# Regrouping the block visits of a fused SwiGLU stage, with a lower initial pace of weight conversion

## The chip, the cores and the metric

The kernel runs on one core of one Trainium2 chip. The metric is device time in microseconds. Three runs of the kernel before took 545.49, 545.72 and 546.81 us; the median is 545.72 us. One further execution was profiled: it took 543.5 us, of which 541.7 us lie between its first and its last instruction (the span). All times of rows below are microseconds from the start of that span.

## The reference, cut to what matters

Three layers follow each other. The first two (chunked attention with a softmax inside each chunk, then a soft mixture of experts) fill the first third of the kernel and are not touched. The third is a SwiGLU layer on 4608 tokens with 512 features and 1536 hidden features:

```python
def _moe2_ref(x, w_gate, w_val, w_out):
    g = x @ w_gate
    silu = g * (1.0 / (1.0 + np.exp(-g)))
    val = x @ w_val
    return (silu * val @ w_out).astype(np.float32)
```

Its x is the output of the mixture, `c @ slot_out` with only 32 slots. The kernel therefore never forms x: it multiplies `slot_out` with the weights once and then works from the 32 combine weights of each token.

## The kernel before, in words

**Blocks, chunks, steps.** The 4608 tokens are nine blocks of 512. The 1536 hidden features are six chunks of 256, and each chunk has two halves of 128, so there are twelve halves f = 0 to 11 (chunk c holds f = 2c and 2c+1). One step handles one block and one half. `emit_gv` (L840) makes two matmuls, gate and value (L847), then ScalarE's Silu (L850) and VectorE's product (L851). `emit_hl` (L854) splits the product in a high part (ScalarE, L859) and a low part (GpSimd, L860). `emit_out` (L866) multiplies both parts with the output weights: for each of four groups of 128 tokens, three matmuls (L891, L892, L893) add into one PSUM tile o0 to o3.

**Visits.** `SCHED` (L29) lists groups of (blocks, chunks). For each group every block of it is visited once, and goes through all halves of the group's chunks. The four PSUM tiles collect over one visit only. At its end they are cleared: on a block's first visit they are copied into an SBUF tile `part` (tiles 1 and 3 by VectorE, L900, tiles 0 and 2 by ScalarE, L902); on each later visit VectorE adds all four into `part` (L904). After the last chunk (f = 11) `part` is written out (L907). PSUM has five such buffers (pool `ps_o`, L795), so the next visit finds one buffer free, and takes the others as they are cleared.

**Order of the work.** The order is written out by hand, and every engine follows it in program order. The main loop (L949) goes over n, the running number of the step. In iteration n stand, in this order: `emit_gv` of step n, `emit_hl` of step n-1, one `conv_step`, and `emit_out` of step n-2, with the clearing of its four tiles if a visit ends there. The clearing of a visit thus stands behind whatever `conv_step` has put on VectorE in the same iteration.

**Weight conversion.** The weights of the SwiGLU layer come as 64-bit floats and are converted on the chip, in 36 units (six chunks, three kinds of weight, two halves). A unit goes through four stages, one per `conv_step`: a (L171; VectorE L186 and L187), b (L191; VectorE L195), c (L198; VectorE L200, then a GpSimd product L213), d (L228; ScalarE L234, then a subtraction L239 that falls to GpSimd and VectorE by turns). `conv_step` (L249) runs what is waiting in the order d, c, b, and then starts a new unit with a, if it may. Line 960 decides that: `36 - len(conv_q)` units have been started, and a new one starts while that is below `RATE * n + R0`, with `RATE` 0.38. With all of a chunk's gate and value units done, `emit_g` (L822) makes the chunk's combined weights (16 matmuls, L828); `conv_until` (L263) would force conversion stages if a step came to its weights before that.

Of the kernel before, what the change touches and what calls it, by code (L numbers as in the profile page):

```python
# [20 lines left out]
NWX = 4  # L21
NSP = 9
RESV = 6
R0 = 7.4
CV_AT = (14,)
LATE = 3
C_AT = (3, 4, 5, 6, 7, 9, 10, 11, 12)
RATE = 0.38
SCHED = [((0, 1, 2, 3, 4), (0,)), ((5, 6, 7, 8), (0, 1)), ((0, 1, 2, 3, 4), (1, 2)), ((5, 6, 7, 8), (2, 3)),  # L29
         ((0, 1, 2, 3, 4), (3, 4)), ((5, 6, 7, 8), (4, 5)), ((0, 1, 2, 3, 4), (5,))]  # L30


@with_exitstack
def tile_attn_softmoe_swiglu(
# [214 lines left out]
    def conv_step(start=True):  # L249
        for k, f in (("d", conv_d), ("c", conv_c), ("b", conv_b)):  # L250
            if stage[k]:
                f()
        if start and conv_ready():
            conv_a()
# [13 lines left out]
    with tc.manual_schedule():  # L268
# [646 lines left out]
        seq = []  # L915
        for blocks, cs in SCHED:
            for b in blocks:
# [31 lines left out]
        for n in range(len(seq) + LAG):  # L949
# [9 lines left out]
            if 1 <= n < len(seq):  # L959
                conv_step(36 - len(conv_q) < RATE * n + R0)  # L960
            if n > LAG:
# [57 lines left out]
```

## Time and profile before

| | us |
|---|---|
| median of three runs | 545.72 |
| profiled execution | 543.5 |
| its span | 541.7 |
| TensorE busy | 521.3 (96% of the span) |
| VectorE busy | 406.7 (75%) |
| ScalarE busy | 260.4 (48%) |
| GpSimd busy | 252.9 (47%) |

A matmul row lasts longer than the distance to the next one, because matmuls overlap in the engine: in an undisturbed step they start 0.23 us apart while each row shows 0.39 us. The distance between starts is therefore the measure of TensorE's speed, and an idle time in a row is shorter than the delay by the overlap. VectorE's rows show the same in small: a row of 0.67 us is followed by the next after 0.60 us. The clock column gives the granted share of TensorE's full clock.

### The profile page before, as it was taken

Reading aid. Unit: us, or ns where it says so; the run is one execution under the profiler, and the core shown is the slowest. Engines: PE = TensorE matmul, PEld = TensorE weight load, DVE = VectorE, ACT = ScalarE, POOL = GpSimd, SP = SyncE. Lnnn points to the kernel's source line nnn. Section 1 sums busy time; section 2 is a strip of 40 time slices with the busy share of each in tenths; the row PEclk is TensorE's granted clock in tenths of the full one; section 3 lists DMA queues with packets and bytes.
Section 4 is the critical chain, followed back from the end, with each engine's and each line's share of the span. In section 5 each row is a group of like instructions: output and inputs, shape, how many; then the busy total and the mean of one; then the engine's idle time right before and its main releaser. Section 6 shows DMA issues by size and latency. Waiting matters only on the chain.

```text
span 541.7 us, 11039 instructions
## 1 busy us (share of the span) xinstructions
PE 521.3 (96%) x4389; PEld 409.8 (76%) x4389; DVE 406.7 (75%) x673; ACT 260.4 (48%) x504; POOL 252.9 (47%) x252
## 2 busy tenths in 40 slices
PE   7899999998998889999999999999999999999997
PEld 6778887873335568888888888888888888888885
DVE  5778987864766999888898889989898943433554
ACT  1344533342447766666565555545654533333331
POOL 3333343321002576576566756656664743343342
PEclk9999999999999989999999999999999999999999
DMA  8999999999999502020202220222000000222344
GB/s 324 404 358 398 348 405 347 413 416 400 421 416 417 247 1 77 2 78 2 77 1 77 77 79 0 79 79 77 0 1 0 3 0 1 77 79 77 113 179 174
DMA packets 23762, 91.09 MB, mean 168 GB/s; under 512 B 3104, under 2 KB 3104, under 8 KB 17696
## 3 DMA queue, kind: packets, MB, share of 16 engines
q1 hardware_dynamic: 23712, 90.40, 43.1%
q8 instruction: 34, 0.56, 0.4%
q14 instruction: 16, 0.13, 0.1%
HBM read 80.95 MB, written 9.44 MB: 167 GB/s over the span
## 4 chain that ended last, share of the span: by engine, by line
PE 81%; DVE 9%; DMA 6%; issue 2%; ACT 1%; POOL 0%; SPq 0%; ACTq 0%; DVEq 0%
PE o L891 18%; PE o L893 18%; PE o L892 18%; DMA w2t<-in_moe_w_dram 6%; PE v_ps L847 4%; PE g_ps L847 4%; PE xa_ps L365 4%; PE xt_ps L401 3%; PE s_ps L328 3%; PE pt_ps L351 2%; PE gg_ps L828 2%; PE si_ps L484 1%; DVE ssb L338 1%; DVE m L336 1%; PE h_ps L652 1%
## 5 line engine op out<-in xcount | busy, mean ns | idle before, releaser
L860 POOL TENSOR_TENSOR lo_sb<-s_sb,hi_sb 128x512 fp32r<-128x512 f32 x106 | 140.5, 1326 | 130.9 <-ACT hi_sb L859 127.9
L891 PE MATMUL o<-whl,hi_sb 128*128 128x512 f32 x428 | 167.7, 392 | 2.5 <-DVE part L900 2.5
L893 PE MATMUL o<-whl,lo_sb 128*128 128x512 f32 x428 | 167.2, 391 | 0.5 <-POOL lo_sb L860 0.5
L892 PE MATMUL o<-whl,hi_sb 128*128 128x512 f32 x428 | 167.1, 390 | 0.0
L850 ACT ACTIVATE s_sb<-g_ps 128x512 f32<-128x512 f32 (+1 forms) x110 | 64.7, 590 | 149.9 <-PE g_ps L847 147.7
L851 DVE TENSOR_TENSOR s_sb<-s_sb,v_ps 128x512 f32<-128x512 f32 (+1 forms) x110 | 74.0, 674 | 74.5 <-ACT s_sb L850 73.2
L891 PEld LDWEIGHTS o<-whl,hi_sb 128*128 128x128 f32 x428 | 80.6, 188 | 22.2 <-DVE part L900 4.5
L893 PEld LDWEIGHTS o<-whl,lo_sb 128*128 128x128 f32 x428 | 80.6, 188 | 17.8 <-POOL lo_sb L860 0.9
L892 PEld LDWEIGHTS o<-whl,hi_sb 128*128 128x128 f32 x428 | 80.6, 188 | 16.3
L859 ACT ACTIVATE hi_sb<-s_sb 128x512 fp32r<-128x512 f32 (+1 forms) x110 | 67.6, 616 | 0.8 <-DVE s_sb L851 0.8
L904 DVE TENSOR_TENSOR part<-part,o 128x512 f32<-128x512 f32 x92 | 57.1, 677 | 2.6 <-PE o L893 2.6
L318 POOL COPY vbd<-vbd 64x520 f32<-64x520 f32 x36 | 22.3, 619 | 69.9 <-DMA vbd<-in_v_dram 56.2
L213 POOL TENSOR_TENSOR mt<-mt,ex 128x512 f32<-128x512 f32 x32 | 39.5, 1234 | 27.5 <-PE g_ps L847 13.8
L200 DVE SCALAR_TENSOR_TENSOR ex<-raw,ex 128x512 uint16<-128x512 uint16 x32 | 47.2, 1477 | 0.1
L847 PE MATMUL v_ps<-c_t,g_st 128*128 128x512 f32 (+1 forms) x110 | 42.5, 390 | 0.8 <-DMA raw<-in_moe_w_val_dram 0.5
L847 PE MATMUL g_ps<-c_t,g_st 128*128 128x512 f32 (+1 forms) x110 | 42.4, 389 | 0.1
L353 ACT ACTIVATE pt<-pt_ps 128x512 f32<-128x512 f32 x36 | 19.5, 596 | 36.2 <-PE pt_ps L351 36.2
L195 DVE SCALAR_TENSOR_TENSOR mt<-mt,raw 128x512 f32<-128x512 f32 x32 | 34.9, 1090 | 0.0
L336 DVE TENSOR_REDUCE m<-s_ps 128x16 f32<-128x1024 f32 x18 | 22.0, 1224 | 14.8 <-PE s_ps L328 14.7
L187 DVE TENSOR_SCALAR mt<-raw 128x512 int32<-128x512 int32 x32 | 32.9, 1027 | 0.0
L365 PE MATMUL xa_ps<-vbd,pt 128*64 128x130 f32 x432 | 28.2, 277 | 0.0
L403 ACT ACTIVATE xt<-xt_ps 128x512 f32<-128x512 f32 (+1 forms) x36 | 19.3, 596 | 13.7 <-PE xt_ps L401 10.2
(138 smaller groups left out, 664.2 us busy)
## 6 DMA issues: line engine op xcount, KB each, us to landing
qk<-in_qk_dram SPq DMA_DIRECT2D x36, 512.0 KB, 6.6
w1t<-in_moe_w_dram SPq DMA_DIRECT2D x16, 1024.0 KB, 9.3
w2t<-in_moe_w_dram SPq DMA_DIRECT2D x15, 1024.0 KB, 13.5
vbd<-in_v_dram SPq DMA_DIRECT2D x36, 260.0 KB, 7.5
out_dram<-part SPq DMA_DIRECT2D x36, 256.0 KB, 2.2
raw<-in_moe_w_out_dram SPq DMA_DIRECT2D x6, 1024.0 KB, 7.1
raw<-in_moe_w_gate_dram SPq DMA_DIRECT2D x5, 1024.0 KB, 4.8
raw<-in_moe_w_val_dram SPq DMA_DIRECT2D x5, 1024.0 KB, 5.1
```

Source lines behind the costliest of these rows:

```text
L200: nc.vector.scalar_tensor_tensor(out=ex, in0=hh, scalar=0x8000, in1=ex, op0=ALU.bitwise_and, op1=ALU.bitwise_or)
L213: nc.gpsimd.tensor_tensor(out=m, in0=m, in1=p, op=ALU.mult)
L365: nc.tensor.matmul(out=banks[n // 3][64 * cc:64 * cc + 64, (n % 3) * 2 * VW:(n % 3 + 1) * 2 * VW], lhsT=pt_t[i][:, j, 64 * cc:64 * cc + 64 ...
L847: nc.tensor.matmul(out=ps[:, k], lhsT=g_st[:, c, gi, ff:ff + 128], rhs=c_blk(b)[:, k], start=True, stop=True)
L850: nc.scalar.activation(out=s[:, k], in_=gp[:, k], func=ACTF.Silu)
L851: nc.vector.tensor_tensor(out=s[:, k], in0=s[:, k], in1=vp[:, k], op=ALU.mult)
L859: nc.scalar.activation(out=hi[:, k], in_=s[:, k], func=ACTF.Copy)
L860: eng.tensor_tensor(out=lo[:, k], in0=s[:, k], in1=hi[:, k].bitcast(F32), op=ALU.subtract)
L891: nc.tensor.matmul(out=a, lhsT=hi[:, ts], rhs=w_hi, start=first, stop=False)
L892: nc.tensor.matmul(out=a, lhsT=hi[:, ts], rhs=w_lo, start=False, stop=False)
L893: nc.tensor.matmul(out=a, lhsT=lo[:, ts], rhs=w_hi, start=False, stop=last)
L904: nc.vector.tensor_tensor(out=p[:, t], in0=p[:, t], in1=a, op=ALU.add)
```

## The change

`SCHED` and `R0` change, and nothing else. Before, five blocks pass chunk 0, then four pass chunks 0 and 1, and from then on five and four blocks by turns pass two chunks at a time. After, seven blocks pass chunk 0, two pass chunks 0 and 1, three pass chunk 1 alone, four pass chunks 1 and 2, and then five and four by turns pass two chunks, with four blocks left for chunk 5. The constant of the pace line falls from 7.4 to 6.0.

```diff
-R0 = 7.4
+R0 = 6.0
 CV_AT = (14,)
 LATE = 3
 C_AT = (3, 4, 5, 6, 7, 9, 10, 11, 12)
 RATE = 0.38
-SCHED = [((0, 1, 2, 3, 4), (0,)), ((5, 6, 7, 8), (0, 1)), ((0, 1, 2, 3, 4), (1, 2)), ((5, 6, 7, 8), (2, 3)),
-         ((0, 1, 2, 3, 4), (3, 4)), ((5, 6, 7, 8), (4, 5)), ((0, 1, 2, 3, 4), (5,))]
+SCHED = [((0, 1, 2, 3, 4, 5, 6), (0,)), ((7, 8), (0, 1)), ((0, 1, 2), (1,)), ((3, 4, 5, 6), (1, 2)), ((7, 8, 0, 1, 2), (2, 3)),
+         ((3, 4, 5, 6), (3, 4)), ((7, 8, 0, 1, 2), (4, 5)), ((3, 4, 5, 6), (5,))]
```

## Rows read from the trace of the kernel before

**Rows 1.** Windows: stretch, its length, busy us (x instructions) per engine, clock, DMA share, GB/s.
```profile
192.00:195.60 3.60, 3.46 (x9) 2.69 (x10) 3.17 (x6) 1.17 (x3) 2.25 (x3) 0.55 0.02 5
212.00:280.00 68.00, 68.00 (x307) 56.00 (x306) 59.78 (x70) 44.06 (x78) 42.66 (x33) 1.00 0.12 43
280.00:430.00 150.00, 150.00 (x685) 124.47 (x684) 133.40 (x170) 82.82 (x145) 95.11 (x72) 1.00 0.12 43
```

**Rows 2.** Waits of TensorE from 184 us on: total us, times, longest.
```profile
PE o L891 <- DVE part L900: 2.5, 1, 2.5
```

**Rows 3.** Timeline of TensorE: start, us, line, tiles, form [idle before <-releaser].
```profile
189.21 0.40 PE L893 MATMUL o<-whl,lo_sb 128*128 128x512 f32 x1
192.14 0.63 PE L891 MATMUL o<-whl,hi_sb 128*128 128x512 f32 x1 [2.53 <-DVE part L900]
...
195.55 0.49 PE L891 MATMUL o<-whl,hi_sb 128*128 128x512 f32 x1
195.88 0.39 PE L892 MATMUL o<-whl,hi_sb 128*128 128x512 f32 x1
```

**Rows 4.** Timeline of VectorE ahead of that stall, iterations 2 and 3.
```profile
185.38 0.42 DVE L186 TENSOR_SCALAR ex<-raw 128x512 uint16<-128x512 uint16 x1
185.72 0.42 DVE L187 TENSOR_SCALAR mt<-raw 128x512 int32<-128x512 int32 x1
...
186.65 1.52 DVE L200 SCALAR_TENSOR_TENSOR ex<-raw,ex 128x512 uint16<-128x512 uint16 x1
...
191.40 0.68 DVE L900 COPY part<-o 128x512 f32<-128x512 f32 x1
```

**Rows 5.** Timeline of VectorE, then GpSimd, then TensorE, iteration 15.
```profile
230.34 1.80 DVE L200 SCALAR_TENSOR_TENSOR ex<-raw,ex 128x512 uint16<-128x512 uint16 x1
...
232.40 1.39 DVE L187 TENSOR_SCALAR mt<-raw 128x512 int32<-128x512 int32 x1
233.71 1.27 DVE L900 COPY part<-o 128x512 f32<-128x512 f32 x2
...
232.22 1.29 POOL L213 TENSOR_TENSOR mt<-mt,ex 128x512 f32<-128x512 f32 x1 [0.63 <-PE g_ps L847]
...
228.62 0.39 PE L847 MATMUL g_ps<-c_t,g_st 128*128 128x512 f32 x1
...
234.06 0.39 PE L893 MATMUL o<-whl,lo_sb 128*128 128x512 f32 x1
234.44 0.50 PE L891 MATMUL o<-whl,hi_sb 128*128 128x512 f32 x1
```

**Rows 6.** Timeline of TensorE, then VectorE, iteration 31 and the next visit.
```profile
281.89 0.39 PE L847 MATMUL g_ps<-c_t,g_st 128*128 128x512 f32 x1
...
285.07 0.39 PE L847 MATMUL g_ps<-c_t,g_st 128*128 128x512 f32 x1
...
286.20 0.42 PE L891 MATMUL o<-whl,hi_sb 128*128 128x512 f32 x1
286.46 0.39 PE L892 MATMUL o<-whl,hi_sb 128*128 128x512 f32 x1
...
285.40 2.47 DVE L904 TENSOR_TENSOR part<-part,o 128x512 f32<-128x512 f32 x4
```

**Rows 7.** Timeline of TensorE, then VectorE, iteration 39.
```profile
307.37 0.39 PE L847 MATMUL g_ps<-c_t,g_st 128*128 128x512 f32 x1
...
310.54 2.08 PE L828 MATMUL gg_ps<-whl,so_hl 128*128 128x256 f32 x16
312.45 0.40 PE L847 MATMUL g_ps<-c_t,g_st 128*128 128x512 f32 x1
...
311.65 2.47 DVE L904 TENSOR_TENSOR part<-part,o 128x512 f32<-128x512 f32 x4
```

**Rows 8.** Early gap of TensorE on the timeline, and the window behind it.
```profile
9.01 1.09 PE L351 MATMUL pt_ps<-ident,ssb 128*128 128x128 f32 x8 [1.52 <-DVE ssb L338]
...
9.00:12.50 3.50, 3.49 (x96) 3.25 (x98) 1.22 (x1) 1.08 (x2) 1.50 (x4) 1.00 1.07 384
```

## The prediction

> **What bounds the kernel now.** I began with busy time by stretch. From 212 us to 430 us TensorE is busy all the time at full clock, while VectorE is busy 59.78 of 68 us and 133.40 of 150 us [rows 1]. So the SwiGLU stage runs at TensorE's pace, and VectorE has about a tenth to spare: it does not set the pace on the average, but may at single places. A step is 3.18 us, the distance between the gate matmuls of iterations 31 and 32 [rows 6]; over 14 matmuls that is a pitch of 0.227 us. Next I read TensorE's waits. From 184 us on VectorE appears once, with 2.5 us: a matmul waits for the clearing of a PSUM tile [rows 2]. The timeline puts that wait at 192.14 us, and behind it the matmuls run at 0.43 us instead of 0.227 until 195.6 us, at a granted clock of 0.55 on the mean of that stretch, that is mostly the 1.2 GHz level [rows 1, 3].
>
> Idle time alone hides small delays, since rows overlap. I therefore looked at distances between starts. In iteration 15 one tile's matmul starts 0.38 us after the one before, and its own row is 0.11 us longer than usual [rows 5]: (0.38 - 0.227) + 0.11 = 0.26 us lost. The same pair of distances stands in iterations 7 and 23, so there are three.
>
> **Where conversion and clearing meet.** Both kinds of loss have one cause: in an iteration the clearing stands on VectorE behind that iteration's conversion stages. Which stages those are follows from the pace line. A unit starts in iteration n if fewer than 0.38n + R0 have been started, and six have been started ahead of the loop. Starts come two or three iterations apart. Two apart, a new unit's stage a falls into the iteration of the last one's stage c ("c+a"); three apart, a falls together with a stage d.
>
> Before, a visit ends in iterations 3, 5, 7, 9, 11, and then every fourth one, 15, 19, 23, 27, 31 up to 99. The starts two apart end in 5, 7, 15, 23, 28, 36, 44, 49, 57, 65, 73. So c+a meets a clearing in 5, 7, 15 and 23, all first visits (5 lies in the wake of the long stall and is left out of the sum), and never in a visit that adds.
>
> After, visits end in 3, 5, 7, 9, 11, 13, 15, 19, 23, then 25, 27, 29, and then in 33, 37, 41 and every fourth one. The starts two apart end in 3, 8, 16, 24, 29, 37, 45, 53, 58, 66, 74. So c+a meets a first visit once, in 3, and visits that add four times, in 29, 37, 45 and 53. In 69, d on VectorE and a meet an adding visit; in 27 they do too, but there the chunk's weights follow on TensorE.
>
> **What c+a costs at a clearing.** In iteration 15, L200 ends at 232.14, L187 takes 1.39 us beside GpSimd's product instead of 0.42 us, and the clearing begins at 233.71, 5.09 us after the iteration's gate matmul [rows 4, 5]. On a first visit VectorE's first clearing is that of tile 1, and the rows show the fourth tile of the next visit waiting for it; the loss is 0.26 us. On an adding visit VectorE clears tile 0 first. One buffer is free, so the next visit's second tile waits for tile 0. Iteration 31 shows that limit: clearing begins 285.40 - 281.89 = 3.51 us after the gate matmul, and the next visit's second tile comes 286.46 - 286.20 - 0.227 = 0.03 us late [rows 6]. The second tile stands two tiles, six matmuls, ahead of the fourth, and 6 x 0.227 = 1.36 us. So c+a at an adding visit costs 0.26 + 1.36 = 1.62 us. As a cross-check, by iteration 31 it is 0.03 + (5.09 - 3.51) = 1.61 us. For d and a, iteration 39 begins its clearing 311.65 - 307.37 = 4.28 us after the gate matmul; there 1.91 us of L828 cover it [rows 7]. Without that cover, as in 69, it costs 1.62 - (5.09 - 4.28) = 0.81 us. Stage b or c alone costs nothing in the six adding visits of before that have it, nor does a beside a d on GpSimd beyond the 0.03 us above.
>
> **The change part by part, against the profiled 543.5 us** (541.7 of span and 1.8 around it; the median of the runs, 545.72, is 2.2 higher).
>
> 1. *Lower R0, early.* Iteration 2 no longer starts a unit, and iteration 3 has c and a instead of c, b and a. VectorE loses the L186 and L187 of 185.38 to 186.05 us (0.67 us). Behind L200 only a is left; in iteration 15 clearing begins 1.57 us after L200's end. Set on the L200 of 186.65 + 1.52 = 188.17 us, that gives 189.74, or 189.07 with the 0.67 us, against 191.40 [rows 4, 5]. The waiting matmul starts 0.74 us behind the clearing, at 189.8 to 190.5 instead of 192.14: 1.65 to 2.3 us. L200's start moves up, so I take 2.3. With a shorter idle the clock should stay up: 192.14 to 195.88 us holds nine pitches, 3.74 - 9 x 0.227 = 1.7 us [rows 3]. Gain 4.0; bounds 1.65 (clock still falls) and 2.7 + 1.7 = 4.4 (no stall left, next matmul at 189.44).
> 2. *c+a leaves the first visits* in 7, 15 and 23: gain 3 x 0.26 = 0.8.
> 3. *c+a comes to adding visits* in 29, 37, 45, 53: loss 4 x 1.62 = 6.5. *d and a* in 69: loss 0.8.
> 4. *34 visits instead of 32*, so eight more L904 of 0.6 us (2.47 / 4), 5 us of VectorE [rows 6]. They lie beside TensorE's matmuls; where they are late, it is counted in 3. In 25, 27 and 29 visits end every second iteration; 25 has b alone on VectorE, and 27 is covered by L828. If that cover is short, a visit costs up to 0.8.
> 5. *Later conversion.* Chunk 1's gate and value are done in iteration 11 and needed in 16: 5 x 3.18 = 16 us of cover. Chunks 2 to 5 are done 3, 3, 7 and 7 iterations ahead, so no stage is forced. Each weight load keeps six iterations to its first use, with the DMA share at 0.12 [rows 1]. Nothing.
> 6. *The new waits themselves.* Behind the waiting matmul stand the rest of that `emit_out` and all later steps, so TensorE loses the whole wait. Behind the clearing stands the next L851, some 3 us late; its result is used two iterations on. Nothing more. The tail (two halves, four adds, the last write) is unchanged.
>
> Sum: -4.0 - 0.8 + 6.5 + 0.8 = +2.5 us. That gives 546.0 on the profiled execution and 548.2 on the median. Its own bounds are -4.4 - 0.8 + 6.9 = +1.7 (four waits at 1.51, the mere delay, and 0.8) and -1.65 - 0.8 + 7.3 + 0.8 (item 4) = +5.7; I put its range at 547.3 to 550.7.
>
> **The clock.** TensorE went idle for 1.52 us at 9.01 us, and the window behind it is at 1.00 [rows 8]; 2.53 us were followed by 0.55. The new waits are 1.51 us minus the usual overlap of 0.16, 1.35 us of idle, so I let the clock stay. The Trainium skill (TensorE: Matmul & The Clock Gate, section HAM oscillation) says that idle gaps between bursts of matmuls can send the clock back to its lower level each time; by that rule this change, which brings regular gaps, would be worse than my sum. So far the trace agrees for the longest gap and not for the 1.52 us one.
>
> **The rivals.** *Faster.* The four meetings don't happen, because the starts fall one iteration off my count; from one iteration on all four are missed together. For it: it hangs on one whole number. Against: by the same count the three small losses of before are in 7, 15 and 23, where the trace has them. Time: 545.72 - 4.0 - 0.8 = 540.9. *No change.* The waits form, but L187 runs at 0.42 us because GpSimd's product comes later behind the adds; each wait shrinks by 0.97 us to 0.65: -4.8 + 4 x 0.65 + 0.8 = -1.4, 544.3. Against: L187 has 1.39 in iteration 15. *Slower by the clock.* Each of the four long waits takes 1.7 us more: 548.2 + 6.8 = 555.0. *Conversion late.* One forced unit in front of chunk 1 or 3, about one step: 551.
>
> **How the numbers follow.** About 0.3% (1.6 us) is what a measurement of this kernel can tell from no change: faster means below 544.1, slower above 547.4. My forecast has 0.65 (0.61 slower, 0.04 same), the missed meetings 0.15, the smaller waits 0.14, the clock 0.04, late conversion 0.02. So faster 0.15, same 0.04 + 0.14 = 0.18, slower 0.61 + 0.04 + 0.02 = 0.67. The range runs from 543.5, which takes in the smaller waits, to 550.8; it leaves out the missed meetings and the clock, 0.19 in all. The forecast's own range is 547.3 to 550.7.
>
> **What would show it.** In the waits of TensorE, L891 on the clearing L904: five times, some 6 us, the longest about 1.4, in iterations 29, 37, 45, 53 and 69. The wait on L900 at about 189 us shrinks to near 1 us or less, with full clock behind it. No lost 0.26 us at first visits. If L904 does not appear among the waits, the count of iterations is wrong; if it appears with L187 at 0.42 us, the price is; if the clock column falls behind the waits, the third rival holds.

## The result, and the profile after

The changed kernel is slower. Its median is 548.56 us over 13 runs; the kernel before, run beside it, has 544.87 us over 13 runs. The ratio is 1.0058, with a 95% interval of 1.0035 to 1.0080: about 3.2 us slower (the two medians differ by 3.7 us). The forecast had been 2.5 us slower, 548.2 us.

One execution of the changed kernel was profiled too; it took 550.84 us, with a span of 549.1 us. That is 7.4 us over the span before, more than the medians differ by. Some of it has nothing to do with the change: the first gate matmul of the SwiGLU stage (L847 of step 0) comes at 177.68 us instead of 173.38, in code that is the same. About 2 us of these 4.3 came where the clock was down (last section); the other 2 had come by 113 us, and why was not followed up. So I compare the stretch from that matmul to the end of the span: 541.7 - 173.4 = 368.3 us before, 549.1 - 177.7 = 371.4 us after, 3.1 us more. This stretch is called the stage from here on.

TensorE's waits from 184 us on, of the changed kernel, to be set beside [rows 2] (columns as there):

```profile
PE o L891 <- DVE part L904: 5.9, 5, 1.3
...
PE o L891 <- DVE part L900: 0.9, 1, 0.9
```

L904, which did not appear before, now holds TensorE up five times. The early wait on L900 shrank from 2.5 us to 0.9 us. The timeline of TensorE shows the five places, four alike and one shorter, and the early one last:

```profile
281.25 0.50 PE L891 MATMUL o<-whl,hi_sb 128*128 128x512 f32 x1 [1.34 <-DVE part L904]
...
308.30 0.50 PE L891 MATMUL o<-whl,hi_sb 128*128 128x512 f32 x1 [1.34 <-DVE part L904]
...
337.31 0.50 PE L891 MATMUL o<-whl,hi_sb 128*128 128x512 f32 x1 [1.35 <-DVE part L904]
...
364.40 0.50 PE L891 MATMUL o<-whl,hi_sb 128*128 128x512 f32 x1 [1.34 <-DVE part L904]
...
418.09 0.50 PE L891 MATMUL o<-whl,hi_sb 128*128 128x512 f32 x1 [0.54 <-DVE part L904]
...
194.19 0.50 PE L891 MATMUL o<-whl,hi_sb 128*128 128x512 f32 x1 [0.91 <-DVE part L900]
```

What VectorE does ahead of the first of them is iteration 29's conversion step. The gate matmul of that iteration, on TensorE, is the last row of this fence:

```profile
277.16 1.80 DVE L200 SCALAR_TENSOR_TENSOR ex<-raw,ex 128x512 uint16<-128x512 uint16 x1
278.88 0.41 DVE L186 TENSOR_SCALAR ex<-raw 128x512 uint16<-128x512 uint16 x1
279.22 1.38 DVE L187 TENSOR_SCALAR mt<-raw 128x512 int32<-128x512 int32 x1
280.52 2.47 DVE L904 TENSOR_TENSOR part<-part,o 128x512 f32<-128x512 f32 x4
...
275.44 0.39 PE L847 MATMUL g_ps<-c_t,g_st 128*128 128x512 f32 x1
```

The stages c (L200) and a (L186, L187) stand ahead of the clearing, which begins 280.52 - 275.44 = 5.08 us after the gate matmul; iteration 15 of before had 5.09 us [rows 5]. This is the pattern of before row for row. It now stands in front of a visit that adds, where the next visit's second tile waits for the first clearing.

The lost time can be counted by iteration, as the distance between the gate matmuls of neighbouring steps less 3.173 us (the median step of before) and, where L828 lies between, less 1.91 us. A late clearing in iteration n shows in the distance from n+1 to n+2. Distances over by less than 0.1 us are left out:

| distance from iteration | before | after |
|---|---|---|
| 3 | 0.59 | 0.59 |
| 4, 5 and 6 | 4.14 + 1.13 + 0.12 | 1.41 |
| 8, 16, 24 | 3 x 0.28 | |
| 10 and 26 | | 0.18 + 0.21 |
| 30, 38, 46, 54 | | 1.64 + 1.65 + 1.67 + 1.65 |
| 70 | | 0.83 |
| sum | 6.8 | 9.8 |

The sums differ by 3.0 us, which is the whole of what the stage lost.

Windows behind the early wait and behind the first and the fourth of the long ones (columns as in [rows 1]) show the clock:

```profile
194.20:197.50 3.30, 3.30 (x14) 2.73 (x15) 3.30 (x5) 1.94 (x4) 2.54 (x3) 1.00 0.03 5
281.25:284.50 3.25, 3.25 (x14) 2.71 (x15) 2.94 (x5) 0.94 (x3) 1.74 (x2) 1.00 0.02 5
364.40:367.60 3.20, 3.20 (x14) 2.65 (x15) 3.20 (x6) 0.87 (x3) 0.49 (x1) 1.00 0.60 253
```

It stayed at 1.00, where before it was 0.55 behind the early wait [rows 1].

### The profile page after: what moved, and what is told of

Read it like the earlier page. It is cut to its first block, busy times and chain, and to the rows that moved or that the text cites. A ratio compares the mean times of both kernels' runs of the same rounds, so it can differ in the third digit from the quotient of the medians.

```text
span 549.1 us, 11048 instructions
## 1 busy us (share of the span) xinstructions
PE 524.0 (95%) x4389; PEld 410.0 (75%) x4389; DVE 412.6 (75%) x681; ACT 259.8 (47%) x504; POOL 252.6 (46%) x252
## 4 chain that ended last, share of the span: by engine, by line
PE 85%; DVE 10%; issue 3%; ACT 1%; DMA 1%; POOL 0%; SPq 0%; ACTq 0%; DVEq 0%
PE o L891 17%; PE o L892 16%; PE o L893 16%; PE g_ps L847 4%; PE v_ps L847 4%; PE xa_ps L365 4%; PE s_ps L328 3%; PE xt_ps L401 3%; PE pt_ps L351 3%; PE so_ps L695 3%; PE h_ps L652 3%; PE si_ps L484 2%; PE gg_ps L828 2%; DVE ex L200 2%; PE lt_ps L420 1%
## 5 line engine op out<-in xcount | busy, mean ns | idle before, releaser
L860 POOL TENSOR_TENSOR lo_sb<-s_sb,hi_sb 128x512 fp32r<-128x512 f32 x106 | 140.6, 1326 | 133.8 <-ACT hi_sb L859 130.7
L893 PE MATMUL o<-whl,lo_sb 128*128 128x512 f32 x428 | 166.9, 390 | 0.0
L851 DVE TENSOR_TENSOR s_sb<-s_sb,v_ps 128x512 f32<-128x512 f32 (+1 forms) x110 | 73.9, 674 | 68.2 <-ACT s_sb L850 66.8
L893 PEld LDWEIGHTS o<-whl,lo_sb 128*128 128x128 f32 x428 | 80.4, 188 | 17.2 <-POOL lo_sb L860 0.4
L904 DVE TENSOR_TENSOR part<-part,o 128x512 f32<-128x512 f32 x100 | 62.0, 676 | 2.6 <-PE o L893 2.6
L213 POOL TENSOR_TENSOR mt<-mt,ex 128x512 f32<-128x512 f32 x32 | 38.7, 1210 | 27.9 <-PE g_ps L847 11.9
L200 DVE SCALAR_TENSOR_TENSOR ex<-raw,ex 128x512 uint16<-128x512 uint16 x32 | 44.0, 1375 | 0.1
L847 PE MATMUL v_ps<-c_t,g_st 128*128 128x512 f32 (+1 forms) x110 | 42.3, 388 | 0.8 <-DMA raw<-in_moe_w_val_dram 0.5
L847 PE MATMUL g_ps<-c_t,g_st 128*128 128x512 f32 (+1 forms) x110 | 42.2, 387 | 0.1
L195 DVE SCALAR_TENSOR_TENSOR mt<-mt,raw 128x512 f32<-128x512 f32 x32 | 38.8, 1213 | 0.0
L187 DVE TENSOR_SCALAR mt<-raw 128x512 int32<-128x512 int32 x32 | 34.0, 1062 | 0.0
L365 PEld LDWEIGHTS xa_ps<-vbd,pt 128*64 128x64 f32 x432 | 23.7, 135 | 3.5 <-issue 2.7
```

The source lines that it names most:

```text
L195: nc.vector.scalar_tensor_tensor(out=m, in0=m, scalar=-7.0, in1=lw.bitcast(F32), op0=ALU.add, op1=ALU.add)
L200: nc.vector.scalar_tensor_tensor(out=ex, in0=hh, scalar=0x8000, in1=ex, op0=ALU.bitwise_and, op1=ALU.bitwise_or)
L365: nc.tensor.matmul(out=banks[n // 3][64 * cc:64 * cc + 64, (n % 3) * 2 * VW:(n % 3 + 1) * 2 * VW], lhsT=pt_t[i][:, j, 64 * cc:64 * cc + 64 ...
L847: nc.tensor.matmul(out=ps[:, k], lhsT=g_st[:, c, gi, ff:ff + 128], rhs=c_blk(b)[:, k], start=True, stop=True)
L851: nc.vector.tensor_tensor(out=s[:, k], in0=s[:, k], in1=vp[:, k], op=ALU.mult)
L860: eng.tensor_tensor(out=lo[:, k], in0=s[:, k], in1=hi[:, k].bitcast(F32), op=ALU.subtract)
```

## The experiments

The theory, called the meeting theory below: TensorE waits where two conversion stages on VectorE (c and a, or d and a or b) stand ahead of the clearing of an adding visit in the same iteration. Where that happens follows from the pace line and the visits' lengths alone. The rivals differ by run. All times are of the stage, from each run's own profile, which is one execution.

| run | groups | R0 | conversion step | stage, us | ratio to before, 95% interval |
|---|---|---|---|---|---|
| before | old | 7.4 | | 368.3 | |
| after | new | 6.0 | | 371.4 | 1.0058 (1.0035 to 1.0080) |
| e1 | new | 7.4 | | 377.1 | 1.0190 (1.0148 to 1.0232) |
| e2 | old | 6.0 | | 393.9 | 1.0504 (1.0447 to 1.0560) |
| e3 | new | 6.7 | | 365.3 | 0.9938 (0.9917 to 0.9959) |
| e4 | old | 7.2 | | 375.0 | 1.0116 (1.0077 to 1.0155) |
| e5 | new | 6.0 | behind the clearing | 366.3 | 0.9978 (0.9955 to 1.0001) |
| e6 | new | 6.0 | a ahead of c | 367.1 | one run: 542.97 us |
| e7 | new | 6.7 | behind the clearing | 369.9 | 1.0008 (0.9981 to 1.0034) |
| e8 | old | 7.4 | behind the clearing | 369.9 | 1.0017 (0.9988 to 1.0046) |
| e9 | new | 6.7 | a ahead of c | 366.2 | 0.9952 (0.9928 to 0.9977) |

**The old groups with the pace line moved by 0.2.** If the waits come from the meeting, they can be made in the old groups too, with no visit added.

```diff
 # kernel before
-R0 = 7.4
+R0 = 7.2
```

> The old groups with R0 7.2 instead of 7.4: the first six iterations are those of before, no visit is added, only the pace line shifts, so that c+a meets adding visits in 39, 47, 55 and 63, and d and b in 35. Meeting theory: four waits of L891 on L904 of 1.35 us of idle (1.62 us lost each) and one below 0.8: stretch 368.3 - 0.8 + 6.5 + 0.4, 374 to 375, slower than before by some 6 us though nothing but a constant moved by 0.2. Rival (waits come from the new groups): no wait on L904, 367.5 to 368.5.

TensorE's waits from 184 us on:

```profile
PE o L891 <- DVE part L904: 5.9, 5, 1.3
PE o L891 <- DVE part L900: 2.5, 1, 2.5
```

The first long wait on the timeline, VectorE's rows and then TensorE's:

```profile
311.86 1.39 DVE L187 TENSOR_SCALAR mt<-raw 128x512 int32<-128x512 int32 x1
313.17 2.47 DVE L904 TENSOR_TENSOR part<-part,o 128x512 f32<-128x512 f32 x4
...
313.90 0.50 PE L891 MATMUL o<-whl,hi_sb 128*128 128x512 f32 x1 [1.35 <-DVE part L904]
```

The stage took 375.0 us, at the top of what was expected. The distances from iterations 40, 48, 56 and 64 are over by 1.64 to 1.67 us, that is, the clearings of 39, 47, 55 and 63 were late, as counted, and the one of 35 by 0.79 us. The early wait is untouched. So neither the new groups nor their eight more adds are needed for the waits.

**The new groups without meetings.** The converse: the same visits and adds as after, with a pace line on which c+a never falls on an adding visit.

```diff
 # changed kernel
-R0 = 6.0
+R0 = 6.7
```

> The new groups with R0 6.7: the same visits and the same 100 adds as after, with the pace line shifted so that c+a falls into 9 (a first visit), 14, 22, 30, 38 and so on, and never into an adding visit. Meeting theory: no wait on L904 above 0.1 us, the early wait on L900 short (iteration 3 has c and b): stretch 371.4 - 7.3 and up to 1 us less, 363 to 364.5, which would beat before by some 4 to 5 us. Rival (the added visits cost the time): the five waits stay or move, 370 to 372.

TensorE's waits from 184 us on:

```profile
PE o L893 <- POOL lo_sb L860: 1.5, 2, 1.0
PE v_ps L847 <- ACT s_sb L850: 0.3, 1, 0.3
```

No wait on L904 or L900 of that size is left; the stage took 365.3 us, 6.1 us less than after and 3.0 us less than before. Expected were 363 to 364.5: 0.8 us more than the upper end, and 1.5 us of idle stand in the waits on L860 (GpSimd's low parts) in the first iterations, where conversion is still dense. By its timed runs this is the fastest kernel of the study, 0.62% faster than before (e9 below is not told apart from it). It shows that the added visits cost nothing that can be seen, and that after's loss hangs on one constant.

**Each half of the change alone.**

```diff
 # changed kernel (e1: new groups, old pace)
-R0 = 6.0
+R0 = 7.4
```

> The new groups with R0 left at 7.4. The stretch from the first gate matmul of step 0 to the end of the span is 368.3 us before (541.7 - 173.4) and 371.4 after (549.1 - 177.7); I compare that stretch. Meeting theory (a wait comes where stages c and a fall into the iteration of an adding visit's clearing): iterations 1 to 5 are those of before, so the wait on L900 at the start and the fall of the clock stay; c+a meets adding visits in 49, 57, 65 and 73, d and b in 29 and 45. So four waits of L891 on L904 with 1.35 us each and two smaller ones: 368.3 + 6.5 + up to 1.4, 375 to 376. Rival (the added visits themselves, eight more adds on a full VectorE, cost the time wherever conversion stands): waits gather in iterations 25 to 33, where visits end every second iteration, and the stretch is near 375 as well; only the places differ.

The waits on L904 were six, 6.8 us in total, and the 2.5 us on L900 stayed. The four long ones show in the distances from 50, 58, 66 and 74 (1.63 to 1.67 us each), the counted iterations. The d-and-b meetings of 29 and 45 cost 1.18 and 0.80 us instead of 0.7 at most, and the stage took 377.1 us, 1 us over the expected end. The places, not only the sum, are those of the meeting theory; the rival had the waits between 25 and 33, where of these only the one of 29 stands, which the count had too.

```diff
 # kernel before (e2: old groups, new pace)
-R0 = 7.4
+R0 = 6.0
```

> The old groups with R0 6.0. Meeting theory: the early gain of 4.0 us is there without the new groups, and the three losses of 0.26 us at first visits go. But the old groups need chunk 1's last output weights in iteration 15 and chunk 2's in 31, and conversion stages are forced there, ahead of the clearing: c and then d. No c+a meets an adding visit. Stretch 368.3 - 4.8 + 1 to 3 for the forced stages: 364.5 to 366.5. Rival (new groups are needed for the early gain): 368 or more, with the wait on L900 still at 2.5 us.

This was missed by far: 393.9 us, 27 us over the upper end. The early wait did shrink to 0.9 us, with no regrouping; so far the meeting theory held. But I had priced the forced stages as VectorE time ahead of a clearing. They are a chain that TensorE waits for. TensorE's waits:

```profile
PE o L891 <- ACT whl L234: 13.7, 4, 5.4
PE o L892 <- POOL whl L239: 3.9, 2, 1.9
PE g_ps L847 <- DVE g_st L811: 2.8, 2, 1.4
```

The first three of them on TensorE's timeline, then VectorE, GpSimd and ScalarE ahead of the longest:

```profile
227.24 0.50 PE L891 MATMUL o<-whl,hi_sb 128*128 128x512 f32 x1 [1.67 <-ACT whl L234]
229.68 0.65 PE L892 MATMUL o<-whl,hi_sb 128*128 128x512 f32 x1 [1.94 <-POOL whl L239]
239.93 0.79 PE L891 MATMUL o<-whl,hi_sb 128*128 128x512 f32 x1 [5.41 <-ACT whl L234]
...
235.61 1.77 DVE L195 SCALAR_TENSOR_TENSOR mt<-mt,raw 128x512 f32<-128x512 f32 x1
237.31 0.68 DVE L200 SCALAR_TENSOR_TENSOR ex<-raw,ex 128x512 uint16<-128x512 uint16 x1
...
238.06 1.15 POOL L213 TENSOR_TENSOR mt<-mt,ex 128x512 f32<-128x512 f32 x1 [1.23 <-DVE ex L200]
...
239.25 0.63 ACT L234 ACTIVATE whl<-mt 128x512 fp32r<-128x512 f32 x1 [3.14 <-POOL mt L213]
```

In iteration 15, b, c and d of one unit follow each other through VectorE, GpSimd and ScalarE from 235.6 to 239.9 us, and TensorE can do nothing but wait for the weights; behind it the clock is down as well (0.50 in the window from 239.9 to 243.5 us). The same pair stands at chunk 2. The two halves of the change thus belong together: it is the longer first pass that makes the lower pace possible.

**The clearing ahead of the conversion step.** If only the order inside an iteration makes the clearing late, it can be put first.

```diff
 # changed kernel (e5); with R0 6.7 (e7); the same edit in the kernel before (e8)
-            if 1 <= n < len(seq):
+            ends = n > LAG and seq[n - LAG][3]
+            if 1 <= n < len(seq) and not ends:
                 conv_step(36 - len(conv_q) < RATE * n + R0)
...
                 emit_out(*seq[n - LAG])
+                if ends and n < len(seq):
+                    conv_step(36 - len(conv_q) < RATE * n + R0)
```

> The changed kernel, with one thing moved: in an iteration in which a visit ends, the conversion step stands behind emit_out, so the clearing is first on VectorE. Groups, R0 6.0, and the iterations in which units start stay. The stretch from the first gate matmul to the end was 371.4 us. Meeting theory (the clearing is late only because stages stand ahead of it): the five waits on L904 and the 0.9 us on L900 vanish, 371.4 - 7.4 - 1.2 = 363 us, up to 364. Rival (VectorE is short of time there, the delay moves to the next product L851 and from there to TensorE): waits of the gate or value matmuls on L851 appear, and the stretch stays above 367.

TensorE's waits from 184 us on:

```profile
PE o L893 <- POOL lo_sb L860: 0.9, 4, 0.2
PE gg_ps L828 <- DVE whl L239: 0.3, 1, 0.3
```

One of the places on the timeline of VectorE, GpSimd and TensorE:

```profile
275.50 2.47 DVE L904 TENSOR_TENSOR part<-part,o 128x512 f32<-128x512 f32 x4
277.89 0.68 DVE L200 SCALAR_TENSOR_TENSOR ex<-raw,ex 128x512 uint16<-128x512 uint16 x1
...
278.65 1.29 POOL L213 TENSOR_TENSOR mt<-mt,ex 128x512 f32<-128x512 f32 x1 [1.90 <-DVE ex L200]
279.90 1.47 POOL L860 TENSOR_TENSOR lo_sb<-s_sb,hi_sb 128x512 fp32r<-128x512 f32 x1
...
281.42 0.50 PE L893 MATMUL o<-whl,lo_sb 128*128 128x512 f32 x1 [0.23 <-POOL lo_sb L860]
```

All waits on L904 and L900 are gone: that part of the theory holds. But the stage took 366.3 us, not 363 to 364. Of the 8.6 us that should have gone, 5.1 did. The largest part of the rest came back elsewhere: c now runs behind the clearing, so GpSimd's product L213 runs later, its low part L860 behind that, and four matmuls of L893 wait for it (0.53 us lost each by the distances, 2.1 of the 3.5 us). The others are small: a wait of L828 on L239 (0.57 us by its distance) and 0.1 to 0.4 us at single steps. The rival had the delay move on, but to L851; it moved to L860, and in part only.

> The new groups with R0 6.7 (which alone took 365.3 us for the stretch, with no wait on L904) and the conversion step behind emit_out where a visit ends. Meeting theory: little is left to gain, the wait of 1.0 us on L860 in iteration 6 and 0.4 us at a first visit in iteration 9 may go: 363.5 to 365.5. Rival (the place of the conversion step is worth something by itself): below 362.5.

> The kernel before, old groups and R0 7.4, with only the conversion step put behind emit_out where a visit ends. Meeting theory: the early wait of 2.5 us on L900, the fall of the clock behind it and the three losses of 0.26 us at first visits all come from stages ahead of a clearing, so they go without any regrouping or lower pace: 368.3 - 4.5 - 0.8 = 363, up to 364.5. Rival (the early wait comes from too many conversions in the first iterations, wherever they stand): VectorE is as full, the wait moves to L851 or L860, 366 to 368.

Both took 369.9 us and neither is told apart from before by its timed runs. Both missed their expectations, for two reasons that the rows separate. First, in both profiled executions the clock was low between steps 0 and 2, worth 1.6 us (last section); without that they stand near 368.3. Second, there are new losses that I had not foreseen: e8 has waits on L860 in the first iterations (2.2 us, three times, the longest 1.4 us) where it had that on L900, so the theory's claim for e8, that all of the early loss comes from the clearing's place, is only half right, and the rival's wait on L860 is what came. Dense conversion makes some early wait whichever comes first. In e7 a chunk's weights wait for their last subtraction (L828 on L239, 0.9 us), since units end later in their iteration, and both kernels lose 0.1 to 0.4 us at about a dozen later steps. Putting the clearing first is no free gain: with R0 6.0 it takes 5.1 us off the stage (e5 against after), and with R0 6.7, where no meeting is left to undo, it adds some 3 us beside the clock's 1.6 (e7 against e3). The timed ratios agree: in both pairs the intervals lie apart, e5 below after and e7 above e3.

**What c+a is made of.** The order of stages inside a conversion step, with the clearing still behind them:

```diff
 # changed kernel (e6), and with R0 6.7 (e9): conv_step
-        for k, f in (("d", conv_d), ("c", conv_c), ("b", conv_b)):
-            if stage[k]:
-                f()
+        todo = [f for k, f in (("d", conv_d), ("c", conv_c), ("b", conv_b)) if stage[k]]
+        if stage["d"]:
+            todo.pop(0)()
         if start and conv_ready():
             conv_a()
+        for f in todo:
+            f()
```

> The changed kernel, with stage a of a new unit put ahead of stage c (and b) inside each conversion step; the clearing still stands behind both. It tells what the length of c+a is made of. If L187 is slow (1.39 us instead of 0.42) only because GpSimd's product behind L200 runs at the same time, then a runs beside GpSimd's L860, L200 runs alone at 0.68 us, and the clearing begins 4.1 us after the gate matmul instead of 5.09: four waits of 0.3 to 0.4 us of idle (0.65 lost each), stretch 371.4 - 3.9 = 367.5. If the stages have fixed lengths whatever GpSimd does, the order changes nothing: 1.35 us of idle each, 371.4.

VectorE and GpSimd in iteration 29 (two lines have been added, so L904 is L906 here and L860 is L862), the gate matmul and the waiting matmul of TensorE:

```profile
272.88 1.54 DVE L186 TENSOR_SCALAR ex<-raw 128x512 uint16<-128x512 uint16 x1
274.34 0.41 DVE L187 TENSOR_SCALAR mt<-raw 128x512 int32<-128x512 int32 x1
274.67 0.68 DVE L200 SCALAR_TENSOR_TENSOR ex<-raw,ex 128x512 uint16<-128x512 uint16 x1
275.27 2.47 DVE L906 TENSOR_TENSOR part<-part,o 128x512 f32<-128x512 f32 x4
...
272.84 1.29 POOL L862 TENSOR_TENSOR lo_sb<-s_sb,hi_sb 128x512 fp32r<-128x512 f32 x1 [1.70 <-ACT hi_sb L861]
275.43 1.16 POOL L213 TENSOR_TENSOR mt<-mt,ex 128x512 f32<-128x512 f32 x1 [1.30 <-ACT s_sb L852]
...
271.16 0.39 PE L849 MATMUL g_ps<-c_t,g_st 128*128 128x512 f32 x1
...
276.00 0.50 PE L893 MATMUL o<-whl,hi_sb 128*128 128x512 f32 x1 [0.37 <-DVE part L906]
```

The clearing begins 275.27 - 271.16 = 4.11 us after the gate matmul, 4.1 had been expected, and the four long waits are 0.37 us of idle (0.67 us lost). One of the three instructions, the one that meets GpSimd's L862, is slow; the other two are fast. So 0.97 us of each of after's long waits (1.34 less 0.37) is one of the two places where VectorE and GpSimd were in each other's way; the other is still there, in L186.

> The new groups with R0 6.7 (365.3 us from the first gate matmul to the end, of which 0.9, 1.4 and 0.4 us are lost in iterations 4, 6 and 10) and stage a ahead of c and b inside a conversion step. Meeting theory: no wait on L904, as with R0 6.7 alone, and the loss behind the first visit of iteration 9 (c+a there) goes, since c+a is a microsecond shorter: 364 to 365. Rival (a ahead of the older unit's stages only delays that unit, and so the low parts on GpSimd): new waits on L860 in the first ten iterations, 366 or more.

With R0 6.7 the same order gave 366.2 us instead of e3's 365.3, and the rival was right: the loss from iteration 10 went, but that from 6, a wait on GpSimd's low part, grew from 1.42 to 1.94 us, and small losses appeared in 40 to 62. The timed ratios of e3 and e9 lie inside each other's intervals; which of the two is better is open.

## Why the prediction was right

**The count of meetings** was right in every place: 29, 37, 45, 53 and 69 after. In e4, with the same count by hand, 35, 39, 47, 55 and 63 were right too. This carried the forecast: the rival of the missed meetings, faster, fell.

**The price of c+a** at an adding visit was forecast at 1.62 us and is 1.64 to 1.67; that of d and a in 69 at 0.81 us, and is 0.83. The price was never seen in before. It came from the limit that iteration 31 just touched [rows 6] and the loss in iteration 15 [rows 5], two tiles apart.

**The early gain** was forecast at 4.0 us with bounds of 1.65 and 4.4; the distances from 4, 5 and 6 fell from 5.39 to 1.41 us, by 3.98. The wait ended 2.25 us sooner, counted from step 0 (194.19 - 177.68 = 16.51 against 192.14 - 173.38 = 18.76 us), where 2.3 had been forecast, and the clock stayed up, which gave the rest. That R0 alone does this, and the groups do not, is seen in e2 and e1: the wait on L900 is 0.9 us in e2 and 2.5 us in e1.

**The first visits** gave back 3 x 0.28 us, forecast 3 x 0.26.

**What was mis-sized.** Stage b beside a d on GpSimd in an adding visit (25) costs 0.21 us, and in a first visit (9) 0.18 us; the sum had them at nothing, with 0.8 us as the bound of the former. These 0.4 us, and some hundredths in each long wait, are the distance between +2.5 and the stage's +3.1 us. That the forecast of 548.2 us lies only 0.4 us from the measured 548.56 is in part luck: the median of before that it stood on, 545.72 from three runs, is 544.87 over 13, and the loss was sized too small by about as much. The ends of the range were handled loosely: the sum's own upper bound, +5.7, gives 551.4 us, while the forecast's range stops at 550.7 for no stated reason, and the late conversion at 551 lies outside the wide range (to 550.8), though it was not counted among what that leaves out.

**The clock rival** fell: the four waits of 1.35 us left the granted clock at 1.00. **Late conversion** fell too: from 184 us on no matmul of the changed kernel waits for L234 or L239. **The smaller waits** fell in the changed kernel; e6 shows that their mechanism is real and what it takes to bring it about. That the lower pace costs nothing by itself (step 5) was right with the new groups; e2 shows what it costs without the cover of the longer first pass: more than eight times the loss of the change.

## What to carry to other kernels

On an engine that works in program order, ask of every step that frees a buffer what stands ahead of it in the same iteration; an engine that is 89% busy on the mean can hold up a full one at a few places, and those follow from counting, not from busy shares. When two rhythms (here units every 2.63 iterations and visits every fourth) meet on one engine, a change of either shifts all meetings: try the phase by itself, since a constant moved by 0.2 cost 6.7 us of the stage in the old groups and one moved by 0.7 gained 6.1 us in the new ones. A buffer limit can be priced before it is hit, from an iteration that just touches it and from distances between starts, which show delays too small for the idle column.

## What the runs showed of the hardware

**The clock falls behind the same idle times in one execution and not in another.** Between the first two parts of the kernel the same matmuls run with the same waits in every kernel of this study, and so they do in steps 0 to 2 of the SwiGLU stage. The longest of these waits on the timeline, in the first place before and after, in the second before and in e7:

```profile
123.62 1.08 PE L420 MATMUL lt_ps<-xt,phi_sb 128*32 128x128 f32 x32 [1.02 <-ACT lt_all L453]
...
125.64 1.08 PE L420 MATMUL lt_ps<-xt,phi_sb 128*32 128x128 f32 x32 [1.01 <-ACT lt_all L453]
...
179.25 0.50 PE L882 MATMUL o<-whl,hi_sb 128*128 128x512 f32 x1 [0.99 <-DVE g_st L811]
...
179.88 0.51 PE L882 MATMUL o<-whl,hi_sb 128*128 128x512 f32 x1 [1.00 <-DVE g_st L811]
```

Windows of the kernel before (columns as in [rows 1]) at the two places:

```profile
125.00:135.00 10.00, 8.88 (x70) 3.78 (x70) 5.41 (x27) 2.24 (x9) 1.79 (x7) 1.00 0.99 391
...
178.00:186.00 8.00, 6.72 (x31) 5.13 (x30) 7.61 (x16) 4.62 (x10) 3.15 (x3) 1.00 0.77 317
```

The first of them after the change:

```profile
125.00:135.00 10.00, 8.61 (x67) 4.43 (x67) 3.98 (x15) 2.24 (x11) 1.53 (x5) 0.66 0.91 372
```

The second in e7, whose code there is that of before:

```profile
178.00:186.00 8.00, 6.71 (x22) 4.91 (x23) 7.28 (x15) 4.01 (x11) 3.78 (x3) 0.79 0.92 365
```

The clock is 1.00 in one execution and 0.66 or 0.79 in another, behind idle times of at most 1.02 us. The first place has the fall in after, e1 and e3 and not in the other eight kernels; the second has it in e7 and e8 alone. The twelve waits of 1.34 or 1.35 us in the middle of dense work (after, e1, e4) never moved the clock, and the early wait of 2.53 us was followed by a fall in all three executions that have it (before, e1, e4). The Trainium skill (TensorE: Matmul & The Clock Gate, section HAM oscillation) has idle gaps between bursts of matmuls send the clock down, but the gaps of its example, waits for a DMA, are longer than any of these; the trace agrees that idle gaps can, and shows it behind shorter ones, where the length of a single gap does not decide it. So the prediction had asked more of that section than it says when it set it against the new waits. The falls go with part of the spread of several us between runs of one kernel: in one set of the kernel before (542.75 to 548.55 us), the five runs with a mean granted clock of 0.991 or less took 546.1 to 548.3 us, and the eight with 0.995 or more 542.75 to 545.2 us. This is one reason why a stage is better compared from its own first instruction. What decides whether it falls is open.

**VectorE and GpSimd slow each other, but not where VectorE reads PSUM.** L187 takes 0.41 us alone and 1.38 us beside L213; L200 0.68 us alone and 1.80 us when it starts together with GpSimd's L860. GpSimd's L213 takes 1.16 us beside the adds (e6) and 1.29 us beside L187 [rows 5]. The adds, with one input in PSUM, go at 0.60 us each either way: in eight of the traces, 390 rows of L904 that lie wholly beside a GpSimd instruction and 208 that lie beside none both have a median of 0.68 us. The Trainium skill (GPSIMD Engine Reference, section Key points) names two kinds of VectorE instruction that contend with GpSimd, those in a two-port mode and those with two inputs in SBUF. The rows agree for L200, which has two inputs in SBUF, and for the adds, which have one; whether L187, with one, runs in a two-port mode no row shows.

The loss is no fixed price. GpSimd's rows in iteration 29 of after, beside those of VectorE shown in the section on the result:

```profile
277.12 1.29 POOL L860 TENSOR_TENSOR lo_sb<-s_sb,hi_sb 128x512 fp32r<-128x512 f32 x1 [1.71 <-ACT hi_sb L859]
279.04 1.28 POOL L213 TENSOR_TENSOR mt<-mt,ex 128x512 f32<-128x512 f32 x1 [0.63 <-PE g_ps L847]
```

L200 ends at 278.96, 0.55 us behind the end of L860, and L187 at 280.60, 0.28 us behind the end of L213. In nine of the traces every slow L187 beside L213 (95 rows) ends 0.28 or 0.29 us behind it, and every slow L200 beside L860 (189 rows) 0.55 or 0.56 us behind. So the VectorE instruction looks held until GpSimd's is done, and loses what is left of GpSimd's: about a microsecond where it starts soon behind the other, less where it starts later. Which one is held goes with which starts first: in 26 rows of eight traces L186 starts 0.01 or 0.02 us ahead of L860 and stays at 0.42 us, while L860 takes 1.55 or 1.56 us instead of 1.29.
